# Queries and keys copied through DRAM and transposed before they are split, in an attention and feed-forward kernel

## The chip, the cores and the metric

The kernel runs on one core of one Trainium2 chip. A core has a matrix engine (TensorE, PE in the profile; its weight loads are listed as PEld), three engines for elementwise work (VectorE or DVE, ScalarE or ACT, GpSimd or POOL), and SyncE (SP), which in this kernel issues all DMAs. Each engine works through its own instructions in order and waits on semaphores for the others. TensorE writes its results to PSUM, of which this kernel uses eight banks of 512 float32 columns on 128 partitions; ScalarE and VectorE read them from there. The metric is the device time of one execution in microseconds, lower is better.

## The reference

There are 8 batches of 8 heads with 576 rows of 64 columns. Attention is causal by blocks of 64 rows, and its result goes through a feed-forward network (FFN) with a piecewise quadratic activation:

```python
scores = scale * np.matmul(q, k.transpose(0, 1, 3, 2))       # (8, 8, 576, 576)
mask = block_i >= block_j                                    # blocks of 64
scores = np.where(mask, scores, -1000000000.0)
scores = scores - np.max(scores, axis=-1, keepdims=True)
attn = np.exp(scores)
attn = attn / (np.sum(attn, axis=-1, keepdims=True) + 1e-09)
attn_out = np.matmul(attn, v)
x = attn_out.transpose(0, 2, 1, 3).reshape(B * S, H * D)     # 4608 x 512
h = x @ w_in                                                 # 512 -> 2048
g = np.where(h >= 1, h, np.where(h <= -1, 0.0, (h + 1) ** 2 / 4))
return g @ w_out                                             # 2048 -> 512
```

q, k and v are float32; the two weights come as float64.

## The kernel before

**Precision.** The matrix products run in float32r, which by a comment of the kernel keeps 12 significant bits per operand. An operand x is split into hi = float32r(x) and lo = x - hi, and a product is hi\*hi + hi\*lo + lo\*hi, added up in PSUM.

**Units of work.** Attention works on a pair of heads at a time (`Pair`, L210), 4 pairs a batch, 32 in all. A head's 576 rows are four whole tiles of 128 rows and one last block of 64. The FFN works on chunks of 512 tokens: nine chunks of 16 units, each unit with a first half (`ffn_in`, L584: 12 matmuls, L591) and a second (`ffn_out`, L611: 12 matmuls, L615 and L620). Each unit loads its part of w_out, already split, from DRAM into one of two buffers `wo` (L608).

**Queries and keys.** `load` (L222) brings both heads' rows into one of three buffers `nat`; `split_q` (L260) and `split_k` (L271) make hi and lo of them in SBUF, side by side on each partition, on VectorE (the keys' lo on GpSimd). `turned` (L298) transposes four whole tiles of one head's queries or keys on TensorE (L303). As hi and lo lie side by side, each transposed tile has 64 rows of hi and 64 rows of lo. ScalarE copies them into `qb` or `kb` (L307), where the columns are put back in the order of the rows, one in four at a time, since a partition of `nat` holds four rows that follow one another. A DMA (L313) then moves the hi rows to `qa` or `ka`, whose other rows hold the mask. `turned_last` (L317) does the same for both heads' last blocks, with copies on ScalarE and VectorE (L326, L327). The score product (`product`, L340) is then two matmuls, `qa` with `ka` (hi\*hi and the mask, L345) and `qb` with `kb` (hi\*lo + lo\*hi, L348). `qa`, `qb`, `ka` and `kb` exist once, with room for both heads.

**The rest of the attention.** `scores` (L357) takes the row maximum, exponentials and sums; `turn` (L412) transposes the probabilities, `split` (L407) parts them into hi and lo, and `attn_v` (L494) multiplies by v. In the first batch attention\*v runs unsplit in float32.

**The order.** `attention_steps` (L517) writes out eight steps per pair by hand; the parts of the next pair (`nxt`) are put among those of the current one. Between two steps the main loop (L659) lets the FFN do one half of a unit, from step 36 on; up to then attention runs alone. The float64 weights are converted to float32 and split (`convert`, L139) by ScalarE, VectorE and GpSimd, 24 pieces by step 36 and the other 40 in the FFN's first chunk; each piece is loaded by SyncE (L147). The framework generates the semaphores, and orders the instructions of each engine by priority (the order in which they were written) and by when its own timing model finds them ready, so that an instruction can be issued ahead of an earlier one that isn't ready. Tiles with the same tag share a given number of buffers, and a DMA into one waits for the last reader of what it held.

## Time and profile before

| | |
|---|---|
| time, median of 3 runs | 1313.78 us (1313.12 to 1313.95) |
| profiled execution, first to last instruction | 1305.9 us |
| TensorE busy | 1234.2 us, 95% |
| VectorE busy | 877.9 us, 67% |
| ScalarE busy | 767.2 us, 59% |
| GpSimd busy | 462.9 us, 35% |
| DMA moved | 156.26 MB, 120 GB/s |
| mean granted TensorE clock | 0.978 |

The profiled execution is known by its span of 1305.9 us; the runs' times are longer by 7.9 us and include what lies around the span. A row of a group names the line, the engine, the operation, output<-inputs with shapes and the count; behind the first bar stand busy time in us and mean ns of one instruction, behind the second the idle time before them with what ended it. A row of the timeline begins with the start and the length in us. Matmuls overlap one another, so that their durations add up to more than the time they take. A row of a stage gives its stretch, its length, each engine's busy time with the number of instructions, the granted TensorE clock, the DMA engines' busy share and GB/s.

### The profile page before, as it was taken

To read this page: it belongs to the slowest core of one execution; us is meant where nothing else is said; L and a number is where in the kernel's file an instruction comes from. 1 tells how busy PE (TensorE), PEld (TensorE's weight loads), DVE (VectorE), ACT (ScalarE), POOL (GpSimd) and SP (SyncE) were. 2 spreads that over 40 slices of the span, in tenths; PEclk is the share of its full clock that TensorE was granted. 3 is DMA by queue.
4 is the path that set the end of the run, shared out by engine and by line. 5 is a ranking of instruction groups with operands and counts; after the bars stand their busy time and mean duration, and the time that the engine had idled before them with its cause. 6 is when DMAs were issued, how large, how long until landed. Compare 5 with 4: busy or idle time off the path is not lost.

```text
span 1305.9 us, 19727 instructions
## 1 busy us (share of the span) xinstructions
PE 1234.2 (95%) x6496; PEld 1038.7 (80%) x6496; DVE 877.9 (67%) x2200; ACT 767.2 (59%) x1855; POOL 462.9 (35%) x466
## 2 busy tenths in 40 slices
PE   5878777899999999999999999999999999999998
PEld 4666666688888888888888888888888888888886
DVE  8998989867666777776766766676667676322222
ACT  6887676666666666666666666666666565222222
POOL 3554756632233333323333333322333332222221
PEclk9888898999999999999999999999999999999999
DMA  5655454434333433343333432343334322322322
GB/s 153 186 154 167 160 194 159 156 117 131 108 93 104 140 104 97 104 141 106 107 94 103 141 108 85 106 128 104 103 98 137 108 85 63 126 97 97 129 97 97
DMA packets 113766, 156.26 MB, mean 120 GB/s; under 512 B 55920, under 2 KB 72304, under 8 KB 113664
## 3 DMA queue, kind: packets, MB, share of 16 engines
q1 hardware_dynamic: 113664, 155.01, 38.1%
q8 instruction: 51, 0.84, 0.3%
q14 instruction: 51, 0.42, 0.1%
HBM read 120.59 MB, written 17.83 MB: 106 GB/s over the span
## 4 chain that ended last, share of the span: by engine, by line
PE 74%; DVE 12%; ACT 7%; issue 3%; POOL 1%; DMA 1%; SPq 0%; ACTq 0%; POOLq 0%; DVEq 0%
PE ph L591 28%; PE po L615 16%; PE po L620 8%; PE ps_av L445 7%; PE ps_t L418 5%; PE ps_s L345 3%; PE ps_s L348 3%; PE ps_qk L303 3%; DVE pr L378 2%; ACT pr L372 2%; ACT qb L307 2%; DVE nm L368 2%; DVE work L160 1%; DVE work L154 1%; DVE work L157 1%
## 5 line engine op out<-in xcount | busy, mean ns | idle before, releaser
L606 POOL TENSOR_TENSOR gl<-t,gh 128x512 fp32r<-128x512 f32 x144 | 189.6, 1317 | 617.1 <-ACT gh L605 476.0
L615 PE MATMUL po<-wo,gh 128*128 128x512 f32 x1152 | 298.0, 401 | 0.1
L591 PE MATMUL ph<-xh,wih 128*128 128x512 f32 x576 | 240.0, 417 | 1.0 <-DVE sm L354 1.0
L615 PEld LDWEIGHTS po<-wo,gh 128*128 128x128 f32 x1152 | 208.9, 189 | 39.7 <-ACT gh L605 0.5
L601 DVE SCALAR_TENSOR_TENSOR t<-t 128x512 f32<-128x512 f32 x144 | 108.6, 754 | 186.4 <-ACT t L600 186.3
L591 PE MATMUL ph<-xh,wil 128*128 128x512 f32 x576 | 230.7, 401 | 0.0
L591 PE MATMUL ph<-xl,wih 128*128 128x512 f32 x576 | 228.6, 397 | 0.0
L600 ACT ACTIVATE t<-ph 128x512 f32<-128x512 f32 x144 | 86.1, 598 | 167.1 <-PE ph L591 167.1
L372 ACT ACTIVATE pr<-ps_s,nm 128x128 f32<-128x128 f32 (+3 forms) x256 | 134.2, 530 | 58.3 <-DVE nm L368 58.2
L368 DVE TENSOR_REDUCE nm<-ps_s 128x1 f32<-128x128 f32 (+3 forms) x256 | 123.6, 485 | 60.2 <-PE ps_s L348 59.0
L620 PE MATMUL po<-wo,gl 128*128 128x512 f32 x576 | 155.3, 391 | 0.0
L345 PE MATMUL ps_s<-ka,qa 68*128 68x288 f32 (+4 forms) x384 | 124.7, 339 | 21.1 <-ACT pr L372 11.7
L408 ACT CAST pb<-ps_t 128x512 fp32r<-128x512 f32 (+1 forms) x140 | 77.9, 556 | 105.3 <-PE ps_t L418 81.8
L605 ACT CAST gh<-t 128x512 fp32r<-128x512 f32 x144 | 90.2, 626 | 82.3 <-DVE t L604 80.1
L591 PEld LDWEIGHTS ph<-xh,wil 128*128 128x128 f32 x576 | 110.1, 191 | 23.7
L591 PEld LDWEIGHTS ph<-xh,wih 128*128 128x128 f32 x576 | 110.3, 192 | 21.2 <-DVE sm L354 1.5
L591 PEld LDWEIGHTS ph<-xl,wih 128*128 128x128 f32 x576 | 110.9, 192 | 20.5 <-DVE xl L481 0.2
L620 PEld LDWEIGHTS po<-wo,gl 128*128 128x128 f32 x576 | 108.5, 188 | 23.2
L410 DVE TENSOR_TENSOR pb<-ps_t,pb 128x512 fp32r<-128x512 f32 (+1 forms) x140 | 88.3, 631 | 51.1 <-ACT pb L408 51.1
L348 PE MATMUL ps_s<-kb,qb 128*128 128x288 f32 (+4 forms) x384 | 122.3, 325 | 0.0
L418 PE MATMUL ps_t<-ident_r,pr 128*128 128x128 f32 x640 | 108.6, 286 | 7.0 <-DVE x L468 2.2
L378 DVE TENSOR_SCALAR pr<-pr,sm 128x128 f32<-128x128 f32 (+3 forms) x256 | 109.5, 450 | 3.6
(89 smaller groups left out, 2022.2 us busy)
## 6 DMA issues: line engine op xcount, KB each, us to landing
wo<-wo_split SPq DMA_DIRECT2D x144, 512.0 KB, 3.2
out_dram<-ob SPq DMA_DIRECT2D x36, 256.0 KB, 4.5
qn<-in_q_dram SPq DMA_DIRECT2D x32, 256.0 KB, 2.8
kn<-in_k_dram SPq DMA_DIRECT2D x32, 256.0 KB, 2.9
bits<-in_moe_w_in_dram SPq DMA_DIRECT2D x32, 256.0 KB, 2.8
bits<-in_moe_w_out_dram SPq DMA_DIRECT2D x32, 256.0 KB, 2.9
wo_split<-ws SPq DMA_DIRECT2D x16, 512.0 KB, 2.9
qa<-qb SPq DMA_DIRECT2D x63, 128.0 KB, 2.2
```

What stands on the lines that cost most here:

```text
L345: nc.tensor.matmul(ps, qa[:KA, j, c0 : c0 + P], ka[:KA, j, k0 : k0 + n], start=first, stop=False)
L348: nc.tensor.matmul(ps, qb[:, j, c0 : c0 + P], kb[:, j, k0 : k0 + n], start=False, stop=last)
L368: nc.vector.tensor_reduce(out=nm[:, i : i + 1], in_=ps[:, cs], axis=AX.X, op=ALU.max, negate=True)
L372: nc.scalar.activation(pr[:, cs], ps[:, cs], AF.Exp, bias=nm[:, i : i + 1], scale=1.0, accum_out=sm[:, i : i + 1],)
L378: nc.vector.tensor_scalar_mul(pr[:, cs], pr[:, cs], sm[:, i : i + 1])
L418: nc.tensor.transpose(ps[:, c0 : c0 + P], pr[:, c0 : c0 + P], ident)
L445: nc.tensor.matmul(ps[:, lo_col:], vt, x, start=first and i == 0 and m == 0, stop=last and i == len(parts) - 1 and m == len(mov) - 1,)
L591: nc.tensor.matmul(ph, w[:, cc, fs], x[:, cc, xs], start=(cc == 0 and i == 0), stop=(cc == NCC - 1 and i == 2),)
L601: nc.vector.scalar_tensor_tensor(out=t_, in0=t_, scalar=1.0, in1=t_, op0=ALU.min, op1=ALU.mult)
L606: nc.gpsimd.tensor_tensor(out=gl, in0=t_, in1=gh.bitcast(F32), op=ALU.subtract)
L615: nc.tensor.matmul(po[tt], gh[:, ts_], wo[:, w, :], start=(fc == 0 and w == 0), stop=False)
L620: nc.tensor.matmul(po[tt], gl[:, ts_], wo[:, 0, :], start=False, stop=fc == NFC - 1)
```

## The change

Queries and keys go another way from the input to the rows of `qa`, `qb`, `ka` and `kb`.

- `fetch`, new, issues two DMAs that copy the pair's q and k from the inputs to DRAM tiles `raw`; for the next pair this stands in step 0 of the current one.
- `load` reads q and k from `raw` into one fixed buffer each, `nat["q"]` and `nat["k"]`, of type float32r. Each partition now holds one row of a tile, with head 0's and head 1's 64 columns side by side, in rows of 256 bytes. The pool `att2`, now for v alone, has one buffer in place of three.
- `split_q` and `split_k` are gone.
- `turned` transposes the four whole tiles of both heads at once, unsplit, and `turned_last` the last blocks; `parted` splits the transposed data behind that: hi by ScalarE from PSUM, lo by VectorE from PSUM and hi.
- `placed(j)`, new, brings head j's hi and lo by DMA to their rows: three moves each for queries and keys, and six for head 1's queries, whose last block lies elsewhere: 6 DMAs for head 0 and 9 for head 1, in place of 4 a pair before.
- In the order, the transposes of the next pair's queries and keys are in steps 4 and 5, the last blocks in step 5, `placed(0)` in step 5 and `placed(1)` in step 7. Before, head 0's were transposed in steps 4 and 5, head 1's queries in step 7, and head 1's keys and the last blocks in the pair's own steps 0 and 1.

```diff
-    att2 = ctx.enter_context(tc.tile_pool(name="att2", bufs=3))
+    att2 = ctx.enter_context(tc.tile_pool(name="att2", bufs=1))
...
+    raw = {x: dram.tile([B, H, S, D], F32, tag=f"raw{x}", name=f"raw{x}") for x in "qk"}
...
+    nat = {x: const.tile([P, NTL + 1, 2, D], F32R, tag=f"nat{x}", name=f"nat{x}") for x in "qk"}
...
+        def fetch(self):
+            for name, src in (("q", q), ("k", k)):
+                dst, src = (
+                    x[self.b, 2 * self.hp : 2 * self.hp + 2, :, :].rearrange("h (p s) d -> (h p) (s d)", p=BLK)
+                    for x in (raw[name], src)
+                )
+                nc.sync.dma_start(dst, src)
...
-        def split_q(self):
...
-        def split_k(self):
...
+        def parted(self, name, ps, cols):
+            hi, lo = (x[:, cols] for x in self.hl[name])
+            if name == "q":
+                nc.scalar.mul(hi, ps, SCALE)
+                nc.vector.scalar_tensor_tensor(
+                    out=lo, in0=ps, scalar=SCALE, in1=hi.bitcast(F32),
+                    op0=ALU.mult, op1=ALU.subtract,
+                )
+            else:
+                nc.scalar.copy(hi, ps)
+                nc.vector.tensor_tensor(out=lo, in0=ps, in1=hi.bitcast(F32), op=ALU.subtract)
+
+        def turned(self, name):
+            self.hl[name] = [
+                att1.tile([P, S], F32R, tag=f"{x}{name}", name=f"{x}{name}") for x in "hl"
+            ]
             ps = work_bank("ps_qk")
             for t in range(NTL):
                 nc.tensor.transpose(
+                    ps[:, t * P : (t + 1) * P].bitcast(F32R), nat[name][:, t, :, :], ident_r
+                )
+            self.parted(name, ps[:, :SM], slice(0, SM))
...
+        def placed(self, j):
+            rows_ = slice(j * D, (j + 1) * D)
+            for name, a, bt in (("q", qa, qb), ("k", ka, kb)):
+                hi, lo = (x[rows_].bitcast(F32) for x in self.hl[name])
+                at = [(0, S, 0)] if name == "k" or j == 0 else [(0, SM, 0), (SM, S, BLK)]
+                first, second = (hi, lo) if name == "q" else (lo, hi)
+                for dst, x in ((a[:D], hi), (bt[:D], first), (bt[D:], second)):
+                    for c0, c1, by in at:
+                        nc.sync.dma_start(dst[:, j, c0 + by : c1 + by].bitcast(F32), x[:, c0:c1])
...
             if cur:
                 cur.scores(0, 0)
-                cur.turned(False, 1)
                 cur.load("v")
+            if nxt:
+                nxt.fetch()
...
                 nxt.load("q")
                 nxt.load("k")
-                nxt.split_q()
             yield
-            if nxt:
-                nxt.split_k()
             cur.scores(1, 0)
             cur.turn(0, 2)
             if nxt:
-                nxt.turned(True, 0)
+                nxt.turned("q")
             yield
             cur.scores(1, 1)
             cur.turn_last()
             if nxt:
-                nxt.turned(False, 0)
+                nxt.turned("k")
+                nxt.turned_last()
+                nxt.placed(0)
...
             if nxt:
-                nxt.turned(True, 1)
+                nxt.placed(1)
             yield
```

More of the change, by code (lines that the diff above doesn't have):

```diff
@@ L236, in load @@
                 return
[L237 removed]
             if name == "v":
[L239 to L243 removed]
+                t_ = self.vn = att2.tile([P, 2 * NTL + 2, D], F32, tag="nat", name="vn")
+                whole = [t_[:, j * NTL : (j + 1) * NTL, :] for j in range(2)]
@@ L271, in split_k @@
-        def split_k(self):
-            kn = self.nat.pop("k")[:, : 2 * NTL + 1, :]
-            self.ks = att1.tile([P, 2 * NTL + 1, 2, D], F32R, tag="ks", name="ks")
-            for c0, c1 in ((0, 2 * NTL), (2 * NTL, 2 * NTL + 1)):
-                nc.vector.tensor_copy(self.ks[:, c0:c1, 1, :], kn[:, c0:c1, :])
-            (nc.vector if self.first else nc.gpsimd).tensor_tensor(
-                out=self.ks[:, :, 0, :], in0=kn, in1=self.ks[:, :, 1, :].bitcast(F32),
-                op=ALU.subtract,
-            )
+                    whole[j], src[self.b, h0 + j, :SM, :].rearrange("(t p) d -> p t d", p=P)
+                )
@@ L281, in split_v @@
+            nc.sync.dma_start(last, src[self.b, h0 : h0 + 2, SM:, :].rearrange("h p d -> p h d"))
         def split_v(self):
@@ L284, in split_v @@
                 return
-            vn = self.nat.pop("v")
+            vn = self.vn
             self.vs = []
@@ L539, in attention_steps @@
                 cur.scores(0, 1)
-                cur.turned_last()
             if old:
```

79 lines of the change are left out of this document (21 added, 58 removed).

## The prediction

> **What bounds the kernel now.** I read the busy time by stage first, since the page's shares are a mean over stages, then the chain of work that ended last, then the timeline of one pair of heads on TensorE and on SyncE, then the groups by shape. By stage, the columns being stretch, its length, and busy time and instructions of each engine, then clock, DMA share and GB/s:
>
> ```profile
> core 0: us, PE busy (x) PEld busy (x) DVE busy (x) ACT busy (x) POOL busy (x), PEclk, DMA share, GB/s
> 0.00:118.00 118.00, 86.31 (x446) 68.81 (x446) 103.50 (x309) 93.07 (x259) 57.38 (x77) 0.90 0.57 169
> 118.00:255.00 137.00, 111.52 (x526) 89.71 (x527) 123.67 (x276) 93.40 (x246) 88.19 (x101) 0.90 0.50 164
> 300.00:1050.00 750.00, 745.23 (x4144) 637.24 (x4142) 523.35 (x1350) 473.29 (x1125) 238.04 (x223) 1.00 0.36 110
> 1102.00:1306.00 204.00, 198.47 (x886) 163.82 (x884) 57.89 (x92) 50.59 (x89) 46.77 (x36) 0.99 0.30 104
> ```
>
> Three regimes. Until 255 us VectorE is the busiest (103.5 of 118, then 123.7 of 137) with ScalarE close behind in the first part (93.1 of 118), and TensorE has holes. From about 255 to 1102 us attention and FFN are interleaved and TensorE is busy 745.2 of 750 us (99.4%); VectorE stands at 70%, ScalarE at 63%, GpSimd at 32%. The last 204 us are FFN alone, which the change doesn't touch. The chain of work repeats itself in the middle stage:
>
> ```profile
> 600.24 2.96 PE ph L591 x12
> 634.94 2.96 PE ph L591 x12
> ```
>
> The same group of FFN matmuls comes back after 34.70 us: that is one pair of heads. The 847 us from 255 to 1102 hold 24.4 pairs; the 255 us before them hold the other 7.6 of the 32.
>
> **TensorE: eight transposes fewer per pair.** Before, each head's queries and keys are transposed as hi beside lo, four tiles a time, in four sets (L303); after, both heads stand side by side and two sets do. The two transposes of the last blocks stay. A matmul's duration overlaps the next one's, so the price is the distance from a set's start to the start of what follows it. TensorE in the pair above:
>
> ```profile
> 611.57 0.54 PE L303 MATMUL ps_qk<-ident_r,qs 128*128 128x128 f32 x4
> 611.94 2.08 PE L615 MATMUL po<-wo,gh 128*128 128x512 f32 x8
> ...
> 617.31 0.53 PE L303 MATMUL ps_qk<-ident_r,ks 128*128 128x128 f32 x4 [0.30 <-ACT pr L372]
> 617.68 0.47 PE L591 MATMUL ph<-xh,wil 128*128 128x512 f32 x1
> ...
> 625.66 0.50 PE L303 MATMUL ps_qk<-ident_r,qs 128*128 128x128 f32 x4
> 626.00 0.47 PE L591 MATMUL ph<-xh,wih 128*128 128x512 f32 x1
> ...
> 628.83 0.22 PE L345 MATMUL ps_s<-ka,qa 68*128 68x128 f32 x1
> ...
> 629.30 0.45 PE L303 MATMUL ps_qk<-ident_r,ks 128*128 128x128 f32 x4
> 629.59 0.62 PE L418 MATMUL ps_t<-ident_r,pr 128*128 128x128 f32 x4
> ```
>
> The four sets take 0.37, 0.37, 0.34 and 0.29 us, 1.37 in all; half of that, 0.685 us, times 24.4 pairs is **-16.7 us**. TensorE is saturated there, so I count all of it. The second set shows in its bracket 0.30 us of idle time; I leave that wait standing, since the new sets need a bank too.
>
> Two sentences of the Trainium skill would give other sums. "TensorE: Matmul & The Clock Gate", Part 4, has a 128x128 transpose at about 275 ns in a kernel; by that the saving would be an estimated 8 x 0.275 x 24.4 = 54 us, but here the starts lie 0.37 / 4 = 0.09 us apart, and the trace disagrees. "Perfetto Trace Analysis", Identifying the Most-Contended Engine, says that matmul busy time is a bad measure of headroom and that the busy share of the weight loads is the good one; that is 637.2 of 750 us, 85%, and by it the saving could vanish into slack. In the last 204 us, with FFN alone, the share is 80% and matmuls are no less dense, so I read the 85% as no headroom; a rival below keeps the case.
>
> **ScalarE, VectorE, GpSimd.** The groups (busy time and mean ns behind the bar):
>
> ```profile
> L307 ACT CAST kb<-ps_qk 128x512 fp32r<-128x512 f32 x64 | 69.9, 1092 | 15.2 <-PE ps_qk L303 12.7
> L307 ACT CAST qb<-ps_qk 128x512 fp32r<-128x512 f32 x64 | 69.3, 1082 | 1.0 <-PE ps_qk L303 0.3
> L408 ACT CAST pb<-ps_t 128x512 fp32r<-128x512 f32 x84 | 51.1, 608 | 29.7 <-PE ps_t L432 23.5 <-PE ps_t L418 6.2
> L410 DVE TENSOR_TENSOR pb<-ps_t,pb 128x512 fp32r<-128x512 f32 x84 | 57.2, 681 | 2.5 <-ACT pb L408 2.5
> L276 POOL TENSOR_TENSOR ks<-kn,ks 128x576 fp32r<-128x576 f32 x31 | 44.6, 1437 | 3.3 <-DVE ks L275 2.2 <-DMA vs<-in_v_dram 0.9
> L266 DVE SCALAR_TENSOR_TENSOR qs<-qn,qs 128x576 fp32r<-128x576 f32 x32 | 24.1, 754 | 0.1
> L275 DVE CAST ks<-kn 128x512 fp32r<-128x512 f32 x32 | 15.0, 469 | 0.2 <-DMA kn<-in_k_dram 0.2
> L265 DVE TENSOR_SCALAR qs<-qn 128x512 fp32r<-128x512 f32 x32 | 14.3, 447 | 0.0
> L275 DVE CAST ks<-kn 128x64 fp32r<-128x64 f32 x32 | 7.9, 248 | 0.7
> L265 DVE TENSOR_SCALAR qs<-qn 128x64 fp32r<-128x64 f32 x32 | 6.5, 204 | 0.0
> ```
>
> ScalarE: four copies a pair with scattered columns (2 x 1.092 + 2 x 1.082 = 4.35 us) become two straight ones out of PSUM, the like of L408's 0.608: 1.22 us, so -3.1 us a pair. VectorE: the splits in SBUF (0.447 + 0.204 + 0.754 + 0.469 + 0.248 = 2.12 us) become two subtractions from PSUM, the like of L410's 0.681: 1.36 us, so -0.76 us a pair. GpSimd: -1.44 us. The small copies and subtractions of the last blocks go one for one, and I count them at nothing. From 255 us on all this is worth nothing either: TensorE covers it, and the three engines have 30% and more to spare. Before 255 us it counts. VectorE, the bound: 0.76 x 7.6 = **-5.8 us**. ScalarE's scattered copies stand on the chain of the first 120 us:
>
> ```profile
> by line: issue 8.6%; DVE pr L378 6.3%; DVE work L154 6.0%; ACT kb L307 5.9%; ACT pr L372 4.6%; DVE nm L368 4.6%; ACT qb L307 4.2%; DVE work L160 3.6%; POOL work L166 3.6%; PE ps_t L432 3.4%; ACT pb L408 2.6%; DMA bits<-in_moe_w_in_dram 2.3%
> ...
> 58.35 2.22 DMA ka<-kb
> ```
>
> 5.9% + 4.2% of 120 us is 12.1 us, of which 1.22 / 4.35 = 28% would stay. Between nothing (VectorE late instead) and the full -8.7 I take half: **-4.4 us**.
>
> **The queue of DMAs on SyncE.** Per pair it issued 6 loads of q and k and 4 moves of hi rows (besides 3 for v); it will issue 2 copies DRAM to DRAM, 6 loads, and 6 + 9 moves into the rows: 23 for 10.
>
> ```profile
> 605.46 1.13 SPq L255 DMA_DIRECT2D qn<-in_q_dram  x2
> ...
> 618.97 0.48 SPq L313 DMA_DIRECT2D ka<-kb  x1
> 624.65 0.33 SPq L608 DMA_DIRECT2D wo<-wo_split  x1
> ...
> wo<-wo_split SPq DMA_DIRECT2D x144, 512.0 KB, 3.2
> out_dram<-ob SPq DMA_DIRECT2D x36, 256.0 KB, 4.5
> qn<-in_q_dram SPq DMA_DIRECT2D x32, 256.0 KB, 2.8
> qa<-qb SPq DMA_DIRECT2D x63, 128.0 KB, 2.2
> ```
>
> Thirteen more issues at about 0.5 us are 6.5 us of 34.7; SyncE has room for it. Bytes: two copies of 295 KB and twelve moves of 147 KB in place of four of 131 KB, +1.84 MB a pair, 53 GB/s over the 110 of the middle stage. At 0.36 of the engines' time for 110 GB/s an estimated share of 0.53 results; in the first 118 us (26 us a pair) 169 GB/s become 240 and the share some 0.8. Transfers will be slower there, with no row for it.
>
> New waits on SyncE, in its order. The loads of q and k wait for their copy to land; it is issued three steps (13 us) earlier, and a landing between 2.2 us (a move) and 4.5 us (a store to DRAM) leaves cover: nothing. The moves of head 0 wait for ScalarE's and VectorE's last split; behind them stand the loads of wo (L608), and for those waits ffn_out. The wo load issued at 624.65 is used a whole FFN unit later, after two steps of 4.3 us, and lands in 3.2 us, so a delay of 5 us is covered. The moves of head 1 wait also for the last scores of head 1, one step earlier; their reader comes four steps later. Single buffers in place of three for v, and one for the natural rows and the splits, are free again six steps before their next write: nothing.
>
> What does lengthen is the way from the keys' transposes to head 0's scores: a VectorE subtraction (+0.68), the last block's split (+0.5) and five more issues (+2.4), less 0.48 for the shorter copy and 1.44 for the GpSimd split that came ahead of the transposes: +1.7 us. In the middle stage it is covered (rival below). In the first 255 us the old move (58.35, `ka<-kb`) stands on the chain once in four pairs; 1.7 x 7.6 / 4 = **+3.2 us**, between 0 and 12.9.
>
> **Start.** Before, the first scores begin at 13.10 us:
>
> ```profile
> 13.10 0.48 PE L345 MATMUL ps_s<-ka,qa 68*128 68x128 f32 x1 [3.49 <-DVE ka L309]
> ```
>
> After: the copy of q is issued at about 1.2 and lands, taking 2.9 from between the DMA rows, at 4.1; three loads of q (0.56 each) are out at 5.8, three of k at 7.5, k is there 2.8 later at 10.3; transposes, copy, subtraction (0.37 + 0.61 + 0.68) 12.0; last block 12.5; six moves at 0.48 and a landing of 2.2: 17.6 us. That is **+4.5 us**; with the copy's landing at 2.2 or 4.5 it is +3.8 or +6.1. Weights can be converted meanwhile, which I don't count.
>
> **Sum.** -16.7 - 5.8 - 4.4 + 3.2 + 4.5 = -19.2 us. The profiled execution spans 1305.9 us; the runs' median of 1313.8 lies 7.9 above, launch and end, which stay. 1313.8 - 19.2 = **1294.6 us**.
>
> **Rivals.**
>
> *Head 0's rows come late in the middle stage (slower).* The order on each engine's queue is the framework's, from its modelled times. If it puts the wo load of 624.65 ahead of head 0's moves, SyncE holds them until ffn_out releases the buffer: 624.65 + 0.33 + 6 x 0.48 + 2.2 = 630.1, while the scores begin at 628.83. TensorE then loses 1.2 us a pair, 30 us in all: 1324. It decides from 0.8 us a pair on (19.2 / 24.4). For it: SyncE is one queue in order. Against it: the move at 618.97 went ahead of that wo load, and the moves would be issued by 622.6 then, landing 4 us early; TensorE has FFN work to put ahead.
>
> *The early stage gives back its gain.* With the queue and the DMA engines fuller before 255 us, head 0's rows are late in every pair, not one in four: +9.7, 1304.
>
> *More is gained.* Rows never late early on (-3.2), the scattered copies wholly on the chain (-4.3), and the bank wait of 0.30 gone with fewer banks taken (-7.3): 1280.
>
> *TensorE has slack.* The -16.7 goes and 1311 remains, the case of the weight loads' share. *Transposes at the long price*: 1258, the other page's figure worked through.
>
> **Chances.** Forecast 0.50; late rows in the middle 0.21; early stage gives back 0.15; more gained 0.08; slack 0.04; long transposes 0.02. Runs of this kernel spread over 0.06%, and 0.2% (2.6 us) is what can be told from no change. Faster 0.74, same 0.05, slower 0.21. The range, 1280 to 1325, takes in all but the ends, about 0.86; the forecast's own is 1286 to 1303.
>
> **What the profile after would show.** Transposes in sets of four at the same 0.09 us, 8 + 2 a pair, and TensorE still 99% busy in the middle, with a pair in 34.0 us: the main term right. TensorE idle before L345's successor, released by a DMA into ka or kb, would show the first rival; a FFN that begins later than before, the second. Wrong altogether if the pair stays at 34.7 us or the first 255 us grow by more than 10.

## The result, and the profile after

The changed kernel takes 1329.07 us (median of 4 runs, 1328.4 to 1336.45) beside 1313.57 us for the kernel before on the same chip: ratio 1.0132, 95% interval 1.0108 to 1.0157. It is 1.3% slower, where 1294.6 us was forecast, and it lies above the range. The profiled execution spans 1326.6 us. That is 20.7 more than the 1305.9 of before, while the medians differ by 15.5. Wherever the time and the span of one run are both on record, the time is 1.7 to 2.2 us longer; the profiled execution of before, at an estimated 1305.9 + 1.8 = 1307.7 us, was thus itself quicker than its median. Some 5 us of what follows are the luck of that execution; kernels below whose first pairs have the very instructions of before show how much (end of the experiments).

Busy time by stage of the changed kernel, columns as in the prediction:

```profile
core 0: us, PE busy (x) PEld busy (x) DVE busy (x) ACT busy (x) POOL busy (x), PEclk, DMA share, GB/s
0.00:118.00 118.00, 69.71 (x327) 54.94 (x327) 73.23 (x231) 62.74 (x188) 31.86 (x54) 0.89 0.72 188
118.00:255.00 137.00, 104.93 (x471) 81.27 (x470) 105.08 (x255) 80.82 (x230) 67.98 (x85) 0.87 0.67 189
300.00:1050.00 750.00, 742.59 (x4019) 630.97 (x4020) 527.51 (x1314) 420.29 (x1101) 200.20 (x215) 1.00 0.62 171
1122.00:1326.00 204.00, 199.35 (x890) 164.54 (x888) 58.74 (x93) 51.00 (x89) 46.77 (x36) 1.00 0.32 106
```

From 300 us on nothing is worse: TensorE busy 99%, and a pair is shorter. Two pieces of the chain of waits, the same group one pair apart:

```profile
664.34 2.96 PE ph L588 x12
...
698.31 2.96 PE ph L588 x12
```

33.97 us in place of 34.70. In the first 118 us every engine does less than before: VectorE 73.2 us in place of 103.5, ScalarE 62.7 in place of 93.1, TensorE 69.7 in place of 86.3. In part that is only because fewer pairs fall into the window; but no engine is busy for more than 62% of it; they wait. Where the first score matmuls of a pair start gives the account:

| stretch | before | after | difference |
|---|---|---|---|
| first scores of pair 0 | 13.1 | 16.1 | +3.0 |
| pair 0 to pair 4 | 87.8 | 114.2 | +26.4 |
| pair 4 to pair 8 | 181.8 | 189.6 | +7.8 |
| pair 8 to pair 31 | 796.5 | 780.6 | -15.9 |
| pair 31 to the end of the span | 226.7 | 226.1 | -0.6 |

So the gain came as forecast and the early stage took more than twice as much back. One distance that became longer there is seen in two rows a pair: the transposes of the keys, and the first scores behind them. TensorE before, pair 4 (keys of head 0, then the scores that need its rows):

```profile
95.96 0.81 PE L303 MATMUL ps_qk<-ident_r,ks 128*128 128x128 f32 x4
...
100.85 0.29 PE L345 MATMUL ps_s<-ka,qa 68*128 68x128 f32 x1
```

and after, pair 3:

```profile
88.69 0.81 PE L299 MATMUL ps_qk<-ident_r,natk 128*128 128x128 f32 x4
...
100.68 0.53 PE L342 MATMUL ps_s<-ka,qa 68*128 68x128 f32 x2
```

4.9 us before, 12.0 after. I call this the **way**, and the time from one pair's first scores to the next pair's key transposes the **front**; the two add up to a pair. Means over pairs 1 to 4: before, front 17.2 and way 4.75; after, front 17.45 and way 11.1. The way grew by 6.35 us a pair, and that is 25.4 of the 26.4 us. These are distances between rows of TensorE, though, and not waits: what stands in between is for the framework's order to decide, and that changed too (below).

What lies on this way, first in the chain of waits of the changed kernel (start, us, what):

```profile
77.75 4.26 DMA rawq<-in_q_dram
...
84.33 3.44 DMA natk<-rawk
87.77 0.73 POOL work L169
...
89.02 0.73 POOL ws L173
89.75 0.70 POOL work L169
...
90.47 0.02 ACT ws L171
...
90.78 0.59 ACT hq L283
91.38 0.32 ACT pb L405
...
91.71 0.33 SPq L199
```

then on SyncE's own timeline:

```profile
91.71 0.33 SPq L199 DMA_DIRECT2D wo_split<-ws  x1
92.08 0.43 SPq L150 DMA_DIRECT2D bits<-in_moe_w_out_dram  x1
92.56 1.01 SPq L150 DMA_DIRECT2D bits<-in_moe_w_in_dram  x1
93.67 0.50 SPq L324 DMA_DIRECT2D qa<-hq  x1
...
96.19 0.83 SPq L324 DMA_DIRECT2D kb<-lk  x1
97.07 0.62 SPq L324 DMA_DIRECT2D kb<-hk  x1
```

and ScalarE's, in between:

```profile
91.74 0.60 ACT L289 CAST hk<-ps_qk 128x512 fp32r<-128x512 f32 x1
92.22 0.45 ACT L155 ACTIVATE work<-bits 128x256 f32<-128x256 f32 x1
92.56 0.43 ACT L156 ACTIVATE bits<-bits 128x256 int32<-128x256 uint32 x1
92.88 0.22 ACT L283 ACTIVATE hq<-ps_qk 128x64 fp32r<-128x64 f32 x1
```

Keys transposed at 88.69; ScalarE takes the splits up at 90.78, after casts of the weights' conversion that wait for GpSimd (+2.1); the last block's hi part of q, for which the first move waits too, comes at 92.88 behind the start of another conversion, and SyncE is at a load of weights until 93.57, so that the first of head 0's moves is issued at 93.67 (+2.9); the sixth at 97.07 (+3.4); the scores start at 100.68 (+3.6).

But it isn't the landing of these moves that the scores are shown to wait for. The chain goes past them:

```profile
92.56 5.85 DMA bits<-in_moe_w_in_dram
98.43 0.43 ACT work L155
...
99.44 0.50 ACT pb L405
99.98 0.81 PE ps_av L442 x2
100.79 0.42 PE ps_s L342 x2
```

That is the load of weight bits from SyncE's rows above, its conversion on ScalarE, and, behind it in ScalarE's order, a copy of probabilities that attention\*v waits for on TensorE; the scores stand behind that in TensorE's order. In the kernel before, 6 transposes of probabilities and 8 matmuls of attention\*v stand between a pair's last scores of 512 columns and the next pair's first scores, in each of these four pairs; in the changed kernel there are 7 to 9 and 14 to 20. So a part of the longer way is work that came behind the first scores before.

What TensorE waits for from 16 to 130 us (who waits for whom: us in total, times, longest), before, the first two rows:

```profile
PE ps_t L432 <- DVE sm L354: 7.5, 3, 3.8
PE ps_t L432 <- ACT ws L168: 2.7, 1, 2.7
```

and after, the first five:

```profile
PE ps_qk L299 <- DMA natq<-rawq: 10.1, 4, 3.4
PE ps_t L415 <- DVE pr L375: 8.3, 8, 1.7
PE ps_s L342 <- DMA ka<-hk: 6.0, 1, 6.0
PE ps_t L435 <- DVE sm L351: 5.7, 2, 2.9
PE ps_t L435 <- DVE pr L401: 5.7, 2, 3.2
```

The 6.0 us for a move are the start, ahead of pair 0. From pair 0's first scores to pair 4's TensorE is idle 17.9 us before and 37.1 after, and none of that is put down to a move into `qa`, `qb`, `ka` or `kb`. The largest part is the queries' transposes waiting, once a pair, for rows that are loaded from the copy; most of the rest waits for VectorE. TensorE is also busy longer there, 77.2 us in place of 69.9 with 18 matmuls fewer, at a granted clock of 0.84 in place of 0.90.

### The profile page after: what moved, and what is told of

Read it like the earlier page. It is cut to its first block, busy times and chain, and to the rows that moved or that the text cites. A ratio compares the mean times of both kernels' runs of the same rounds, so it can differ in the third digit from the quotient of the medians.

```text
span 1326.6 us, 19680 instructions
## 1 busy us (share of the span) xinstructions
PE 1221.6 (92%) x6240; PEld 1018.7 (77%) x6240; DVE 848.7 (64%) x2103; ACT 682.9 (51%) x1791; POOL 388.1 (29%) x435
## 4 chain that ended last, share of the span: by engine, by line
PE 68%; DVE 13%; DMA 6%; ACT 5%; issue 4%; POOL 3%; SPq 1%; ACTq 0%; POOLq 0%; DVEq 0%
PE ph L588 25%; PE po L612 15%; PE ps_av L442 8%; PE po L617 7%; PE ps_t L415 4%; PE ps_s L342 3%; PE ps_s L345 3%; DVE nm L365 2%; POOL work L169 2%; DVE t L598 2%; DMA bits<-in_moe_w_in_dram 2%; DVE pr L375 2%; ACT t L597 1%; DVE lq L284 1%; PE ps_qk L299 1%
## 5 line engine op out<-in xcount | busy, mean ns | idle before, releaser
L597 ACT ACTIVATE t<-ph 128x512 f32<-128x512 f32 x144 | 86.1, 598 | 163.6 <-PE ph L588 160.7
L415 PE MATMUL ps_t<-ident_r,pr 128*128 128x128 f32 x640 | 109.6, 285 | 14.3 <-DVE pr L375 8.5
L345 PE MATMUL ps_s<-kb,qb 128*128 128x288 f32 (+4 forms) x384 | 118.8, 326 | 0.1
L375 DVE TENSOR_SCALAR pr<-pr,sm 128x128 f32<-128x128 f32 (+3 forms) x256 | 101.0, 416 | 4.9
```

The lines of the kernel that those rows point to most:

```text
L345: nc.tensor.matmul(ps, qb[:, j, c0 : c0 + P], kb[:, j, k0 : k0 + n], start=False, stop=last)
L375: nc.vector.tensor_scalar_mul(pr[:, cs], pr[:, cs], sm[:, i : i + 1])
L415: nc.tensor.transpose(ps[:, c0 : c0 + P], pr[:, c0 : c0 + P], ident)
```

## The experiments

Each ran beside the kernel before on the same chip, whose median was 1309.3 to 1312.6 us. Front, way and "0 to 4" (from the first scores of pair 0 to those of pair 4) are read from TensorE's rows as above, of one profiled execution each. Four executions that have the same instructions up to pair 4 (before, e15, e17 and e21) took 87.8, 90.1, 91.4 and 93.4 us from pair 0 to pair 4, so differences of up to some 6 us in the last column aren't told apart.

| kernel | us | ratio [95%] | front | way | 0 to 4 |
|---|---|---|---|---|---|
| before | 1313.6 | 1 | 17.2 | 4.75 | 87.8 |
| changed | 1329.1 | 1.0132 [1.0108, 1.0157] | 17.45 | 11.1 | 114.2 |
| e1 no copy | 1326.7 | 1.0130 [1.0105, 1.0154] | 15.25 | 12.25 | 110.0 |
| e3 moves by ScalarE | 1414.2 | 1.0796 [1.0767, 1.0825] | 24.55 | 10.0 | 138.2 |
| e4 before, more issues | 1309.7 | 0.9993 [0.9980, 1.0007] | 17.7 | 5.4 | 92.2 |
| e5 small moves | 1317.0 | 1.0040 [1.0024, 1.0056] | 19.6 | 6.4 | 103.8 |
| e6 bits by GpSimd | 1341.5 | 1.0237 [1.0215, 1.0259] | 24.4 | 9.8 | 136.8 |
| e8 hi by VectorE | 1339.4 | 1.0220 [1.0192, 1.0248] | 18.1 | 12.2 | 121.1 |
| e9 a step earlier | 1335.2 | 1.0185 [1.0163, 1.0207] | 16.25 | 12.45 | 114.9 |
| e10 head 0 small | 1318.0 | 1.0059 [1.0038, 1.0079] | 19.6 | 6.8 | 105.5 |
| e12 head 0 by engines | 1347.2 | 1.0278 [1.0258, 1.0298] | 22.3 | 5.15 | 109.7 |
| e13 changed, 10 pieces | 1347.3 | 1.0277 [1.0256, 1.0299] | 15.8 | 10.1 | 103.6 |
| e14 before, 10 pieces | 1310.7 | 1.0004 [0.9993, 1.0015] | 16.1 | 5.15 | 84.9 |
| e16 e1, e10, e13 together | 1314.2 | 1.0021 [1.0009, 1.0033] | 15.8 | 4.75 | 82.4 |
| e18 changed, casts by GpSimd | 1332.9 | 1.0178 [1.0151, 1.0206] | 17.1 | 12.4 | 118.2 |
| e19 before, casts by GpSimd | 1311.2 | 1.0001 [0.9992, 1.0010] | 17.2 | 5.7 | 91.4 |
| e20 e12 and e13 together | 1344.8 | 1.0242 [1.0222, 1.0263] | 17.8 | 4.05 | 87.3 |
| e15 mixed, no copy | 1300.9 | 0.9932 [0.9907, 0.9957] | 16.95 | 5.6 | 90.1 |
| e17 mixed, with copy | 1290.5 | 0.9846 [0.9826, 0.9866] | 17.6 | 5.2 | 91.4 |
| e21 mixed from pair 5 | 1294.2 | 0.9866 [0.9852, 0.9881] | 17.55 | 5.8 | 93.4 |

**First: one obvious cause each.** The theories in the expectations are Q (SyncE's queue with the added issues sets the early pace), T (the added bytes do) and E (the engines' order, with the splits now behind the transposes, does). e1 loads q and k straight from the inputs, into tiles of float32, and transposes them as float32:

```diff
-            src = {"q": raw["q"], "k": raw["k"], "v": v}[name]
+            src = {"q": q, "k": k, "v": v}[name]
...
-        first.fetch()
...
-            if nxt:
-                nxt.fetch()
```

> The changed kernel without the copy through DRAM: q and k are loaded straight from the inputs, and the whole tiles are transposed as plain float32, which the probabilities' transposes already are. Theory Q (the early stage is a loop through SyncE's one queue in order: copy, wait for its landing, loads, wait for the split, 15 moves, loads of v, next copy, 28 to 30 us a pair where 22 were enough): 2 issues and the wait for the copy's landing go, some 4 us a pair over 8 or 9 pairs, so 1290 to 1298. Theory T (traffic: the DMA engines are too full, all landings are late): 0.6 of the 2.4 MB a pair that come on top go, a quarter of the 37 us lost, so about 1320. Theory E (the split behind the transposes makes a longer way over ScalarE and VectorE): no change, 1329.

2 us less as they stand, 0.3 by the ratios, and within the interval: the copy alone isn't it, and theory Q's gain of 30 us and more did not come. TensorE's wait for the load of the queries fell from 10.1 to 1.4 us, but its waits for VectorE's probabilities (L375) rose from 8.3 to 12.6. e3 issues the moves on ScalarE:

```diff
-                        nc.sync.dma_start(dst[:, j, c0 + by : c1 + by].bitcast(F32), x[:, c0:c1])
+                        nc.scalar.dma_start(dst[:, j, c0 + by : c1 + by].bitcast(F32), x[:, c0:c1])
```

> The changed kernel with the 15 moves a pair issued by ScalarE in place of SyncE; the same bytes and the same waits. Theory Q: some 10 us leave SyncE's loop, the early stage falls back to about 22 us a pair, less what ScalarE pays for the issues and for waiting on VectorE: 1292 to 1305. Theory T: same bytes, 1329. Theory E: 1329 or more.

85 us more than the changed kernel, in all stages (TensorE's busy share from 300 to 1050 us falls to 707.5 of 750): what stands behind the moves in ScalarE's order now waits with them; in those 750 us ScalarE is idle for 82.9 us ahead of the FFN's activation (L597), which the profile puts down to the moves `qb<-lq`. Q falls. e5 cuts the moves to 16 columns:

```diff
                     for c0, c1, by in at:
+                        c1 = c1 if self.first else c0 + 16
```

> The changed kernel with every move cut to 16 columns from the second pair on (the scores are then of stale columns; what is left out is 15/16 or more of the moved bytes, not the number of issues or waits). Theory Q: the issues stay, so 1322 to 1329. Theory T: 1.7 MB a pair go, which is three quarters of what came on top, so 1295 to 1303. Theory E: 1325 to 1329.

12 us come back, between the theories. e4 gives the kernel before thirteen more tiny DMAs a pair on SyncE, six behind the next pair's keys and seven behind its second queries:

```diff
                 nxt.turned(False, 0)
+                more_issues(6)
...
                 nxt.turned(True, 1)
+                more_issues(7)
```

> The kernel before with 13 more DMAs a pair on SyncE's queue, 6 and 7 at the steps where the moves of the changed kernel stand, each of 64 x 16 float32 between two spare tiles. Theory Q, issues alone: 7 us of SyncE's time a pair, with the loads behind them; slower by 5 to 25 us, 1319 to 1339. Theory T: no bytes to speak of, 1313 to 1316. Theory E: 1314.

Nothing: issue slots alone, with nobody waiting for them, cost nothing that is measured here. (In the trace they stand one at a time between the other DMAs, and not in a block as the moves do.) None of the three theories as put survives.

**Second: where on the way.** L is lateness of head 0's rows, W the place of the weights' loads and conversions in the queues, T as before. e9 moves the next pair's loads, transposes, splits and head 0's moves up by one of the eight steps:

```diff
             cur.scores(0, 2)
             cur.turn(0, 0)
+            if nxt:
+                nxt.load("q")
+                nxt.load("k")
             yield
...
             cur.turn(0, 2)
             if nxt:
-                nxt.turned("q")
+                nxt.turned("k")
+                nxt.turned_last()
+                nxt.placed(0)
```

> The changed kernel with the next pair's loads of q and k, both transposes, the splits and the moves of head 0 all one step earlier in the pair's eight steps (the moves then come right behind the last scores of the current pair's head 0, the earliest place that they can have); nothing is added or left out. Theory L (what is lost is lateness: in the first five pairs nothing but the way load, transpose, split, moves, scores sets the pace, and it became longer than the pair): a step of some 3.5 us more cover a pair gives back 10 to 20 us, 1307 to 1317. Theory T (the bytes and packets of the moves): within 3 us of the changed kernel, 1324 to 1330. Theory W (the weights' loads and conversions stand behind the moves in SyncE's order, and the splits behind the conversions in ScalarE's): the same work in another order, 1322 to 1330, or slower.

The front lost 1.2 us and the way gained 1.35: writing it earlier doesn't bring the scores earlier. e10 cuts head 0's moves only:

```diff
                     for c0, c1, by in at:
+                        c1 = c1 if self.first or j else c0 + 16
```

> The changed kernel with head 0's moves cut to 16 of 576 columns from the second pair on, head 1's whole (the output isn't the reference's: most of head 0's transposed rows are left out). Both heads' cut gave 12 us back. Theory L: only head 0's rows are late, so nearly all of it, 1316 to 1320. Theory T: half of it, 1321 to 1325. Theory W: what counts is when the weights' loads behind the moves land; half of it or less, 1321 to 1329.

By the ratios, 9.6 of e5's 12 us are head 0's: not bytes in general (T), but these six moves. Whether it is by their landing isn't shown: with them cut, the framework's order has changed as well, with 0 to 2 matmuls of attention\*v's second group (those that read `pb`) ahead of the first scores, where the changed kernel has 6 to 10; and TensorE's waits for the load of the queries stay, at 11.8 us. Pair 3 of e10:

```profile
86.84 0.81 PE L299 MATMUL ps_qk<-ident_r,natk 128*128 128x128 f32 x4
...
95.12 0.52 PE L343 MATMUL ps_s<-ka,qa 68*128 68x128 f32 x2
```

8.3 us in place of 12.0. But the front grew by 2.1 us as the way shrank by 4.3. The cut moves, with 4 KB of 144, still take 1.7 to 2.7 us to land (medians by tile, from 16 to 130 us), where whole ones took 2.4 to 5.0 in the changed kernel. The Trainium skill ("DMA: Bandwidth & Descriptors", Anatomy of one DMA) states for GpSimd's way of issuing a fixed part of about 2 us that is mostly completion. These moves, issued by SyncE, behave much alike: with a 36th of the bytes, the least median is only 0.7 us lower. e6 and e8 take up W, with the loads of weight bits on GpSimd's queue and with the hi parts made by VectorE:

```diff
-        nc.sync.dma_start(bits, source.bitcast(I32).rearrange("p (n t) -> p n t", t=2))
+        nc.gpsimd.dma_start(bits, source.bitcast(I32).rearrange("p (n t) -> p n t", t=2))
```

> The changed kernel with the loads of the weights' bits issued by GpSimd in place of SyncE, so that they no longer stand behind the moves, and the moves no longer behind them. Theory W: 10 to 25 us back, 1304 to 1319. Theory L and theory T: within 5 us of the changed kernel, 1322 to 1331 (GpSimd has 42 and 81 us of work in the first 118 and the next 137 us, and its issues come on top).

```diff
-                nc.scalar.mul(hi, ps, SCALE)
+                nc.vector.tensor_scalar_mul(hi, ps, SCALE)
...
-                nc.scalar.copy(hi, ps)
+                nc.vector.tensor_copy(hi, ps)
```

> The changed kernel with the hi parts of q and k (four writes a pair) made by VectorE in place of ScalarE, so that they no longer stand behind the conversions' casts on ScalarE that wait for GpSimd, and no hand-over lies between hi and lo. Theory W as far as it is ScalarE's order: 8 to 15 us back, 1312 to 1320. Theory L: the 1 to 3 us a pair that hi waits there and the hand-over come off the way in the first five pairs, 5 to 12 us back, 1316 to 1323. Theory T: nothing, 1325 to 1330. VectorE has the room: 73 of 118 us busy.

Both cost 10 to 14 us more: e6 has a front of 24.4 us, e8 a way of 12.2. I read it as pieces taken out of one in-order queue and put into another where more waits for them; that isn't traced, and e6 has another difference: by pair 4's first scores 34 weight pieces have been through VectorE's part of their conversion there, 23 in the changed kernel. W as one queue's order falls.

**Third: take the moves away, thin the conversions.** e12 lets ScalarE and VectorE write head 0's rows straight from the transposes:

```diff
-                nc.scalar.mul(hi, ps, SCALE)
...
+            for to, rows_ in ((a[:D, 0, cols], slice(0, D)), (bt[at : at + D, 0, cols], slice(0, D)), (hi[D:], slice(D, P))):
+                nc.scalar.mul(to, ps[rows_], scale)
...
-                nxt.placed(0)
```

> The changed kernel with head 0's rows written by ScalarE and VectorE straight from the transposes (hi twice, lo once, for q and k), so that head 0 has no moves; head 1 keeps its nine. Six more engine writes of 64 partitions a pair, some 0.6 us each. Theory L (the pace of the early pairs is set by the way from the transposes to head 0's rows, of which six issues and a landing are 5 to 7 us): as with head 0's moves cut short or better, 1310 to 1318. Theory W (SyncE's, ScalarE's and VectorE's orders, with the weights' conversions in them, set the pace): the added engine work stands in the same orders, 1322 to 1335.

The way is as short as before the change (5.15), and the pair is hardly shorter: the front is 22.3. In the middle stage the added writes make TensorE wait, 726.87 of 750 us busy, 35.2 us a pair. e13 and e14 begin 10 in place of 24 weight pieces ahead of the FFN, in the changed kernel and in the kernel before:

```diff
-    EARLY = 24
+    EARLY = 10
```

> The changed kernel with 10 in place of 24 weight pieces begun before the FFN starts. Read by the distance of the first scores of pairs 1 to 4, 28.6 us on average in the changed kernel and 22.0 in the kernel before. Theory W: with less than half the conversions in the way the distance falls to 23 to 25 us. Theory L: it stays at 26.5 to 29. The time as a whole may rise by the conversions that come later, by 0 to 20 us.

> The kernel before with the same edit, as the measure for the one above. Distance of the first scores of pairs 1 to 4: VectorE, busy 88% there, loses 14 of 24 conversions of some 2 us, 26 us in four pairs, so 17 to 20 us in place of 22 if it sets the pace. Theory W: changed less before is then no more than 4 us a pair; theory L: 7 us or more.

The pairs 1 to 4 gain 2.65 us each in the changed kernel, 0.7 in the kernel before. But the same edit didn't thin the same work. It moves the pieces in the order in which the program writes them, and the framework issued many of them ahead of that: by pair 4's first scores VectorE has done its part of 23 pieces in both kernels, of 10 in e13, and still of 20 in e14. Per piece that is 10.6 / 13 = 0.8 us and 2.9 / 3 = 1.0 us; the spread of like executions makes both rough, but nothing says that a piece costs less in the kernel before. So e14 isn't the measure that e13 needs, and the two don't decide between L and W; what e13 shows is that 13 pieces fewer are worth 10.6 us in the changed kernel. TensorE's wait for the load of the queries all but goes there too, from 10.1 to 0.7 us. Both give it back behind pair 5, where the other pieces are converted (the changed kernel with 18 us more in all). The rows of e14 say something on my forecast as well:

```profile
0.00:118.00 118.00, 87.77 (x454) 71.35 (x455) 98.19 (x302) 88.50 (x245) 45.83 (x65) 0.88 0.51 148
118.00:255.00 137.00, 108.56 (x511) 86.10 (x510) 118.30 (x271) 93.09 (x245) 87.38 (x102) 0.91 0.52 171
```

VectorE loses 5.3 of 103.5 us and the pace moves by 0.7 us a pair. From pair 0's first scores to pair 4's it has 6.8 us less to do, and they come 2.9 us sooner.

**Fourth: do the parts make one chain?** e16 is e1, e10 and e13 at once (no DRAM copy, head 0's moves cut, 10 pieces), e20 is e12 and e13. S says that the parts are links of one chain.

> The changed kernel with three edits at once: no DRAM copy, head 0's moves cut to 16 columns from the second pair on (the output isn't the reference's: most of head 0's transposed rows are left out), 10 weight pieces before the FFN in place of 24. From the first scores of pair 0 to those of pair 4 the changed kernel takes 114.2 us, the three edits alone 110.0, 105.4 and 103.6, the kernel before 87.8 and with 10 pieces 84.9. Theory S (one chain runs through a pair, load, transposes, conversions in the way, splits, moves, and each edit takes its piece out): the pieces add up, 114.2 - 4.2 - 8.8 - 10.6 = 90.6, so 88 to 94 us. Theory R (another thing sets the pace, and each edit only shifts waits): 98 to 105 us.

> Head 0's rows written by the engines (no moves for head 0) and 10 weight pieces before the FFN in place of 24. With the rows written by the engines alone, the keys' transposes came 4.4 to 7.8 us ahead of the next scores, as in the kernel before, but 18.8 to 24.8 us behind the last ones, in place of 15.3 to 18.7. Theory S (what ran beside the longer way, the conversions, now stands ahead of the transposes): with fewer conversions that part falls to 14 to 19 us, and from pair 0's first scores to pair 4's it takes 80 to 92 us in place of 109.7. Rival (the six added engine writes fill that part): 98 to 108 us.

82.4 us in e16, below S's sum, and 87.3 in e20: with the copy and most of the bytes of head 0's moves gone and the conversions thinned, the first four pairs take no longer than in the kernel before; e20 does it without leaving anything out. That doesn't show that the early loss is gone, since e16 and e20 have done 10 and 9 pieces by then and the kernel before 23. At the 0.8 to 1.0 us a piece from above, a rough estimate for the kernel before at 10 pieces is 75 to 77 us, so that 5 to 12 us of the loss would remain. In e16 the last pair of the four reads

```profile
92.56 0.60 PE L299 MATMUL ps_qk<-ident_r,natk 128*128 128x128 f32 x4
...
97.69 0.69 PE L343 MATMUL ps_s<-ka,qa 68*128 68x128 f32 x2
```

5.1 us of way and 18.2 of front. At 10 pieces, copy and moves are worth 103.6 - 82.4 = 21.2 us; at 24 pieces each alone gave 4.2 (within the spread) and 8.7. I read that as the conversions filling in behind: e12 and e20 have fronts of 22.3 us with 24 pieces and 17.8 with 10. e18 and e19 ask whether it is the weights' casts on ScalarE:

```diff
-        nc.scalar.copy(hi(), w32)
+        nc.gpsimd.tensor_copy(hi(), w32)
```

> The changed kernel with the weights' casts to hi made by GpSimd in place of ScalarE. ScalarE then no longer stands twice per conversion pair waiting for GpSimd, ahead of the splits of q and k in its order. Theory W (the splits queue behind those casts): the distance from the first scores of pair 0 to pair 4 falls by 1.5 to 3 us a pair, to 102 to 108 us, the time to 1311 to 1321. Theory S without W: within 3 us of 114.2 and of the changed kernel's time.

> The kernel before with the same edit. ScalarE, 93 of 118 us busy there, loses 24 casts of 0.4 us, GpSimd gains them. All theories: 87.8 us from the first scores of pair 0 to pair 4 becomes 82 to 88, the time 1300 to 1312.

It isn't: 118.2 us in place of 114.2, and 91.4 before, among the 87.8 to 93.4 of like executions. So which queue carries the conversions into the chain isn't settled; e6, e8 and e18 each moved one link and none helped.

**Fifth: the change where it pays.** The mixed kernels go the way of before for the first pairs (eight, or five in e21) and the changed way behind them. e15 has neither DRAM copy nor float32r transposes for the late pairs, and transposes their last blocks as 64 rows; e17 and e21 have the change's copy and form.

```diff
+            self.late = b * NPAIR + hp >= 8
...
-            if nxt:
+            if nxt and nxt.late:
+                nxt.load2("q")
+                nxt.load2("k")
+            elif nxt:
                 nxt.load("q")
                 nxt.load("k")
                 nxt.split_q()
...
+            if nxt and nxt.late:
+                nxt.turned2("k")
+                nxt.turned_last2()
+                nxt.placed(0)
+            elif nxt:
                 nxt.turned(False, 0)
```

> The kernel before for its first eight pairs, and the changed kernel's way (without the DRAM copy, transposed as float32) for the 24 others. If all of the loss lies in the first eight pairs, and the 0.70 us a pair is TensorE's alone: 23 x 0.70 = 16 us less than before, 1293 to 1297. If the gain in the middle stage hangs on the late start of the FFN: 1303 to 1313.

> The kernel before for its first eight pairs and the changed kernel's way for the other 24, now with the DRAM copy and the float32r transposes of the change (the mixed kernel without them had 34.34 us a pair in the middle stage, the changed kernel 33.99). With 33.99 a pair: 23 x 0.71 = 16 us less than before, 1291 to 1296. If the price of a pair in the mixed kernel has another cause than the transposes' form: 1298 to 1303.

> The mixed kernel with the DRAM copy and the kernel before's way for the first five pairs in place of eight, so that pairs 5, 6 and 7, which run beside the FFN's first chunk and its weight conversions, go the changed way. From pair 5's first scores to pair 8's it took 142.8 us with eight, 154.3 in the changed kernel and 148.0 in the kernel before. If the changed way loses there by itself: 150 to 155 us, and 8 to 12 us more in all, 1298 to 1303. If the changed kernel lost there only what the late start of the stage had left over: 141 to 146 us, 1288 to 1293.

e17 is 1.5% faster than the kernel before (ratio 0.9846, 0.9826 to 0.9866) and beats both; its 1290.5 us are 0.5 below its forecast. From pair 8 to pair 31 it takes 14.3 us less than before, from pair 4 to pair 8 5.2 less, which I can't explain. Its chain of waits in the middle, one pair apart, is the changed kernel's:

```profile
516.63 2.81 PE ph L674 x12
...
550.60 2.81 PE ph L674 x12
```

e15, at 34.37 us a pair, misses its forecast of 1293 to 1297 by 4 us: the five transposes of a pair's keys, last block included, take 0.74 us of TensorE's time a pair there, 0.46 in the changed kernel (mean of 16 pairs), where q and k are read from the copy and the last blocks are whole. e21 took 140.6 us from pair 5 to pair 8, where the changed kernel took 154.2 and e17 142.8: pairs 5 to 7 don't lose by the changed way itself. They don't gain by it either: the next pair takes 37.5 us in e21 and 34.1 in e17, and the whole, 1294.2, lies 1 us above its forecast and 3.7 above e17. The 7.8 us of pairs 4 to 8 in the table above I put down to the pairs ahead: the last weight piece is converted at 312 us in the changed kernel, at 255 in the kernel before, 256 in e17 and 270 in e21. Through which queue isn't shown. The first four pairs of e15, e17 and e21 have the instructions of before and took 90.1 to 93.4 us, not 87.8: the profiled execution of before was 2 to 6 us quick there, so of the +26.4 some 21 to 24 are the change, if the one execution of the changed kernel was an ordinary one (its run is 0.7 us below the median).

## Why the prediction was wrong

- **-16.7, TensorE: right.** -15.9 from pair 8 to pair 31 (0.69 us a pair), and e17 realizes it. Over 16 pairs in the middle, the distances from these transposes to what follows add up to 1.50 us a pair before and 0.93 after, so they account for 0.58 of the 0.69; the rest isn't traced. The sets show the same spacing:

```profile
607.67 0.54 PE L299 MATMUL ps_qk<-ident_r,natq 128*128 128x128 f32 x4
608.05 2.08 PE L612 MATMUL po<-wo,gh 128*128 128x512 f32 x8
...
614.27 0.54 PE L299 MATMUL ps_qk<-ident_r,natk 128*128 128x128 f32 x4 [0.24 <-ACT pr L369]
614.64 0.25 PE L308 MATMUL ps_qk<-ident_r,natq 128*128 128x128 f32 x1
```

  0.38 / 4 = 0.095 and 0.37 / 4 = 0.09 us. The rivals "TensorE has slack" and "transposes at the long price" fall with it; so does, here, the rule on the weight loads' share in the Trainium skill ("Perfetto Trace Analysis", Identifying the Most-Contended Engine) as a measure of headroom: 631 of 750 us, 84%, and yet all of the transposes' time came off.
- **-5.8 and -4.4, VectorE's and ScalarE's savings before 255 us: they did not come.** I read "the busiest engine" as "the bound". From pair 0's first scores to pair 4's VectorE is busy 79.4 of 87.8 us before and 74.7 of 114.2 after, ScalarE 73.9 and 67.5: they have less to do in a stretch that became longer, so neither bounds it after the change. Whether VectorE did before stays open: e14 takes 6.8 us of its work out of that stretch, and 2.9 come off the time. ScalarE's casts did not: e19 is without 24 of them, at no change. The Trainium skill ("Perfetto Trace Analysis", Optimization Strategy) tells to look at the gaps in each regime by itself and at what ends them; I did so for the middle stage alone.
- **+3.2, the longer way, with the loads from the copy at nothing: the step that failed.** I put the way at +1.7 us a pair, in one pair of four. With the two savings above, the sum then had the early stage 7.0 us shorter. From pair 0 to pair 4 it became 26.4 us longer, 21 to 24 beside like executions: 5.2 to 6.6 us in each of the first four pairs. My sign for "wrong altogether", 10 us more in the first 255, came with 37 (first scores of pair 8 at 282.7 before, 320.0 after). The place was right, and the distance from the keys' transposes to the scores did grow, by 6.35 us; the mechanism that I had in mind, scores that wait for head 0's rows, isn't what the profile has: TensorE is idle 19.2 us longer in these four pairs, none of it is put down to those moves, and 10.1 us are waits for the load of the queries, which stands behind the copy. I counted the added instructions at their own durations; not counted were the queues that they now join: 2.1 us until ScalarE, in order behind casts, gets to the splits, the conversion and the load of weights that come between them and the first move, and landings under a DMA share of 0.72 (foreseen: 0.8, "with no row for it"). "One in four" came from a chain of before in which `ka<-kb` stands once; the chain of the changed kernel has no move of pairs 1 to 4 in it at all, but a copy (4.26 us), a load from it (3.44) and two loads of weight bits (5.25 and 5.85). How the loss divides among copy, moves, conversions and the changed order stays open: no single edit gave back more than 10.6 us of it.
- **"Thirteen more issues ... SyncE has room": right as such** (e4), wrong as a reason for leaving the queue out. Room in a queue says nothing about who waits at its head: from 16 to 130 us SyncE stands twice, 8.1 us in all, at a store (`wo_split`, L199) that waits for GpSimd, with loads and moves behind it.
- **"Nothing" for the loads' wait on the copy: nearly right for that wait, wrong as a price.** SyncE waits for the copy 1.7 us in all from 16 to 130 us, and the landings there are of 4.0 and 4.1 us (medians). Over all pairs the page's list of DMAs has them above the 2.2 to 4.5 that I allowed:

```profile
rawq<-in_q_dram SPq DMA_DIRECT2D x32, 288.0 KB, 4.8
rawk<-in_k_dram SPq DMA_DIRECT2D x32, 288.0 KB, 4.9
```

  But a copy stands in the chain at 77.75, issued 4.3 us ahead of the load that waits for it, where I had taken 13. Alone it is worth 0.3 to 2 us in all (e1), as other waits fill in; together with the moves, more (e16).
- **+4.5, the start: right in kind,** +3.0; the first copy landed in 3.2 us, 2.9 were taken.
- **The rivals.** "Early stage gives back its gain" had the direction: +9.7 for rows late in every pair, where the first four pairs alone cost 21 to 26. Its mechanism, head 0's rows late, isn't what TensorE's waits show, as said. I had no bound above it, and gave it 0.15. "Head 0's rows come late in the middle stage", to which I gave the slower side, did not occur: that the change came out slower, as this rival had it, bears out nothing of it.
- **The 7.9 us outside the span** were carried over as launch and end. In single runs it is 1.7 to 2.2, so most of the 7.9 was the difference of the profiled execution from the median. The forecast starts at the median and isn't touched by it.

## What to carry to other kernels

Where no engine is busy all the time, as in the first pairs here, look for a chain through the queues; price a change by what it adds from the load to the first dependent instruction, with the wait at the head of every in-order queue that it passes, and count it in every repetition. A saving on a busy engine there can't be counted until an experiment has shown that its time is the pace. A distance between two rows isn't a wait: read who the engine waits for, and what else the order has put in between. An edit of the program isn't yet an edit of the run: count in the trace whether it took out what it should, in the control as well. And a change that pays in one regime and costs in another can be applied to the one alone: the mixed kernel took the middle stage's gain and left the early stage's loss.

## What was not expected of the hardware

- Fifteen moves a pair issued by ScalarE in place of SyncE cost 85 us (e3), and weight loads issued by GpSimd 12 to 14 us (e6), for a kernel in which both engines have idle time. The same DMAs, with the same bytes, were cheaper on the one queue that does nothing else; in e6 the conversions also ran further ahead (34 pieces by pair 4, in place of 23).
- A move of 4 KB lands hardly sooner than a good one of 144 KB (1.7 us beside 2.4, the least medians by tile in e10 and in the changed kernel); what the whole ones cost is the late landings, up to a median of 5.0.
- Transposes as float32 followed each other as closely as float32r ones in the queries' sets, 0.36 us for four to the next group in e1 and 0.38 in the changed kernel, but not in the keys', 0.49 and 0.37 (means of 16 pairs).
